# Weight conversion on VectorE instead of GpSimd, and three attention transposes on TensorE, in an attention and two-MoE kernel

## The chip, the cores and the metric

The kernel runs on one core of one Trainium2 chip. The metric is the device time of one execution in microseconds (us). Three runs of the kernel before took 1321.39 to 1324.82 us, with a median of 1322.66.

A core has a matrix engine (TensorE, PE in the rows), three engines for elementwise work (VectorE = DVE, ScalarE = ACT, GpSimd = POOL) and a queue that issues DMAs (SyncE = SP). Each runs its own list of instructions in order, and they wait for each other through semaphores.

## The reference

```python
# attention: q, k, v are (4, 8, 768, 64); 8 memory keys stand before each window
for c in range(nc):                       # chunks of 32 queries
    c_start, c_end = c * 32, c * 32 + 32
    l_start, r_end = max(0, c_start - 16), min(S, c_end + 8)
    k_full = concatenate([mem_k, k[:, :, l_start:r_end]], axis=2)
    v_full = concatenate([mem_v, v[:, :, l_start:r_end]], axis=2)
    scores = scale * matmul(q[:, :, c_start:c_end], k_full.T)
    a = exp(scores - max(scores))
    out[:, :, c_start:c_end] = matmul(a / (sum(a) + 1e-9), v_full)
x = out.transpose(0, 2, 1, 3).reshape(3072, 512)
# first MoE: 512 -> 2048 -> 512
h = x @ w_in
x = (maximum(h, 0) + log1p(exp(-abs(h)))) @ w_out
# second MoE: 512 -> 1536 -> 512
y = ((x @ w_a) * (x @ w_b)) @ w_out2
```

The weights lie in memory as 64-bit floats; everything else is 32-bit.

## The kernel before

**Numbers in two parts.** A large product is made of three matmuls with operands that are rounded to the type fp32r: high by high, high by low, low by high. So each operand, a weight as well as an activation, is split once: ScalarE copies it into the rounded type (high part), another engine subtracts this from the value (low part). For the activations g of the first MoE that is `split`, with ScalarE at L443 and GpSimd at L444; for x, ScalarE at L317 or L413 and VectorE at L318 or L414.

**Converting a weight.** A tile of 128x512 weights arrives as pairs of 32-bit words (raw). `convert_a` makes a 32-bit float (tmp) of it: ScalarE handles the high words (L104), VectorE shifts the low words (L106) and joins the two (L107). `convert_b` splits that: ScalarE makes the high part (L114), GpSimd the low part (L115). There are two tmp buffers, so the next L106 waits for the L115 two tiles before. 32 tiles belong to the first MoE, 36 to the second.

**Stages.** The 3072 tokens go in 8 tiles of 384. Phase 1 does the attention and the first MoE, phase 2 the second MoE; in between the result x1 is written to memory and read again.

- First the tokens of tile 0 are attended in six blocks of 64 queries (class Block, the table ROUND), while the first weights are loaded and converted. How many loads stand ahead of each block's own loads on SP is in EARLY_RAW, and W_BY has those behind the blocks.
- Then come the tiles t = 0 to 7 of phase 1. Each takes 16 steps f: twelve matmuls make ph (`emit_h`, L454), ScalarE makes three activations of it (L460 to L462), VectorE joins them to g (L464), g is split, and twelve matmuls bring it into four accumulators px (`emit_x1`, L477). px of step f - 2 stands behind ph of step f (LAG = 2), and ph has two banks. So g must be split within about one group of twelve matmuls.
- Meanwhile the next tile's three units of 128 queries are attended (class Unit). A unit's steps are: turn (VectorE transposes k and q with 32x32 stream transposes, L355 to L361, and ScalarE adds the memory keys, L363), scores (TensorE, L374), soft (VectorE's reductions L327, ScalarE's eight exponentials L331), norm (VectorE L335 and L336, then the product L338, for units on GpSimd), flip and flip2 (ten stream transposes by VectorE of the attention weights into af, L392), values (TensorE, L406) and place (x's two parts, L413 and L414).
- During tile 0 the rest of the first MoE's weights are converted too (1.5 tiles per step, CV_AT), and the loads run AHEAD tiles ahead. In the last tile, t = 7, and in phase 2's first tile, it is the second MoE's weights. x for phase 2 is loaded and split in `load_x1` (L491, VectorE L493, GpSimd L494). At the end of a tile the accumulators are copied out (xo, L482) and stored.
- In phase 2 a step makes two groups of twelve (`emit_ab`, L509), their product c (ScalarE L516, VectorE L518), its split, and twelve matmuls into y (`emit_y`, L529).

**What sets the order.** Up to the end of tile 0 each engine's list is just the order in which the code is written. From tile 1 on only TensorE's and VectorE's lists are, the others come from a scheduler, and in phase 2 only TensorE's. A plan places the units: a slot is half a step (2f before px, 2f + 1 behind it), and the tables STEPS and EARLY_STEPS give each step's distance from the unit's place. The three units attended during tile 0 (numbers 3, 4 and 5, here called unit 1, 2, 3) use EARLY_STEPS with a place of their own, EARLY_AT + EARLY_BY * i. SP loads k and q for the next tile after the last unit's turn (L187, L189), and in the last part of tile 0 it also issues the first loads that stay for phase 2.

A unit's attention weights after the softmax (sm) have queries on the 128 partitions and keys along the row; `values` wants keys on the partitions (af), hence the flip. The blocks before tile 0 do this with four transposes on TensorE against an identity matrix, ident (L303), and a copy by ScalarE.

## Time and profile before

| | before |
|---|---|
| median of 3 runs | 1322.66 us |
| the profiled execution | 1324.25 us |
| its span | 1322.4 us |
| TensorE busy | 1242.5 us, 94% |
| VectorE busy | 486.7 us, 37% |
| ScalarE busy | 530.9 us, 40% |
| GpSimd busy | 405.6 us, 31% |

The span goes from the first to the last instruction of the trace; the execution's own time holds 1.85 us more around it. A share of busy time is a mean over stages: tile 0 begins at 50.41 us, tile 1 at 167.17, the last tile at 629.54. From 723.75 on only the second MoE's work is left, where the y of its first step begins. In tile 0 each of the four engines is busy for a half to three quarters of the time; from tile 1 to tile 6 and in phase 2 TensorE is busy nearly all the time and the others for a small part.

### The profile page before, as it was taken

The page shows a single profiled execution, that of the slowest core. Times are in us where ns is not written, and L with a number is a line of the kernel's source. Part 1 is how long each engine was busy: PE and PEld are TensorE (multiplying, and loading weights), DVE is VectorE, ACT ScalarE, POOL GpSimd, SP SyncE. Part 2 cuts the span into 40 slices and gives each one's busy share as a digit, 9 for nine tenths or more (in the row PEclk, how much of TensorE's full clock was granted, in tenths as well). Part 3 has the DMA queues.
Part 4 walks back from the last instruction along what each step waited for, and adds up shares of the span by engine and source line. Part 5 has one row for each costly group of instructions (what it writes and reads, how often), then busy time and mean ns, then how long its engine had stood idle before and what let it go on. Part 6 is the DMA issues. An engine that isn't in the chain of part 4 may idle for free.

```text
span 1322.4 us, 20143 instructions
## 1 busy us (share of the span) xinstructions
PE 1242.5 (94%) x7848; PEld 1173.3 (89%) x7848; DVE 486.7 (37%) x1199; ACT 530.9 (40%) x1322; POOL 405.6 (31%) x348
## 2 busy tenths in 40 slices
PE   5767799999999999999798999999999999999998
PEld 3667789999999999999787999999999999999997
DVE  5677744544444454444778511110111011010100
ACT  4655656556556556554675311111111111111111
POOL 2454522323322322323677521121212121121111
PEclk9688889999999999999999999999999999999999
DMA  8962411213141311311765000010100001000000
GB/s 189 204 215 70 83 42 34 64 27 57 36 73 36 58 50 31 66 22 42 238 201 191 7 25 25 0 48 1 48 1 32 18 0 49 0 24 1 24 1 24
DMA packets 170170, 77.99 MB, mean 59 GB/s; under 512 B 137691, under 2 KB 162395, under 8 KB 170075
## 3 DMA queue, kind: packets, MB, share of 16 engines
q1 hardware_dynamic: 169563, 76.64, 22.0%
q8 instruction: 61, 1.00, 0.3%
q14 instruction: 34, 0.28, 0.1%
q0 software_dynamic: 512, 0.07, 0.0%
HBM read 64.09 MB, written 12.58 MB: 58 GB/s over the span
## 4 chain that ended last, share of the span: by engine, by line
PE 79%; DVE 5%; issue 5%; POOL 4%; SPq 3%; ACT 2%; DMA 1%; DVEq 0%; POOLq 0%; ACTq 0%
PE pab L509 30%; PE ph L454 16%; PE py L529 15%; PE px L477 15%; POOL w L115 3%; DVE tmp L106 2%; DVE tmp L107 2%; PE sc L374 1%; SPq L269 1%; PE pxa L406 1%; ACT w L114 1%; ACT e L461 1%; SPq L266 0%; ACT e L462 0%; SPq L89 0%
## 5 line engine op out<-in xcount | busy, mean ns | idle before, releaser
L509 PE MATMUL pab<-x,w 128*128 128x384 f32 x2304 | 418.9, 337 | 0.3 <-PE px L477 0.3
L509 PEld LDWEIGHTS pab<-x,w 128*128 128x128 f32 x2304 | 405.7, 188 | 9.2 <-PE px L477 0.6
L454 PE MATMUL ph<-x,w 128*128 128x384 f32 x1536 | 299.8, 344 | 16.3 <-ACT x L413 6.8
L454 PEld LDWEIGHTS ph<-x,w 128*128 128x128 f32 x1536 | 273.3, 192 | 23.6 <-ACT x L413 7.8
L518 DVE TENSOR_TENSOR c<-pab,a 128x384 f32<-128x384 f32 x96 | 53.5, 557 | 498.8 <-PE pab L509 497.8
L464 DVE SCALAR_TENSOR_TENSOR g<-ph,e 128x384 f32<-128x384 f32 x128 | 71.1, 556 | 250.5 <-ACT e L462 241.1
L516 ACT COPY a<-pab 128x384 f32<-128x384 f32 x96 | 46.1, 480 | 249.0 <-PE pab L509 249.0
L115 POOL TENSOR_TENSOR w<-tmp,w 128x512 fp32r<-128x512 f32 x68 | 101.5, 1496 | 104.4 <-ACT w L114 74.1
L460 ACT ACTIVATE e<-ph 128x384 f32<-128x384 f32 x128 | 62.0, 484 | 121.4 <-PE ph L454 109.5
L392 DVE STREAM_TRANSPOSE af<-sm 32x256 f32<-32x256 f32 x210 | 91.2, 434 | 3.0
L107 DVE SCALAR_TENSOR_TENSOR tmp<-raw,tmp 128x512 uint32<-128x512 uint32 x68 | 77.5, 1141 | 11.0 <-ACT raw L104 6.8
L106 DVE SCALAR_TENSOR_TENSOR tmp<-raw,zero 128x512 uint32<-128x512 uint32 x68 | 71.8, 1058 | 20.7 <-POOL w L115 18.4
L461 ACT ACTIVATE e<-e 128x384 f32<-128x384 f32 x128 | 67.1, 525 | 3.6
L462 ACT ACTIVATE e<-e 128x384 f32<-128x384 f32 x128 | 67.0, 524 | 3.7
L331 ACT ACTIVATE sm<-sm,st 128x96 f32<-128x96 f32 x168 | 60.5, 362 | 14.5 <-DVE st L327 14.5
L114 ACT CAST w<-tmp 128x512 fp32r<-128x512 f32 x68 | 41.8, 614 | 46.0 <-DVE tmp L107 46.0
L338 POOL TENSOR_TENSOR sm<-sm,st 128x768 f32<-128x768 f32 x21 | 32.2, 1536 | 60.1 <-DVE st L336 46.9
L104 ACT ACTIVATE raw<-raw 128x512 f32<-128x512 f32 x68 | 45.7, 672 | 6.6 <-DMA raw<-in_moe_w_in_dram 4.4
L406 PEld LDWEIGHTS pxa<-af,vn 96*64 96x64 f32 x672 | 23.1, 143 | 19.2 <-DVE af L392 9.7
L406 PE MATMUL pxa<-af,vn 96*64 96x64 f32 x672 | 26.5, 233 | 13.5 <-DVE af L392 9.2
L327 DVE CUSTOM_DVE_ANT_0 sm<-sc,mask 128x96 f32<-128x96 f32 x168 | 31.4, 252 | 6.5 <-PE sc L374 6.5
L374 PEld LDWEIGHTS sc<-kt,qt 64*64 64x64 f32 x672 | 17.2, 147 | 18.1 <-DVE x L414 7.5
(220 smaller groups left out, 1883.5 us busy)
## 6 DMA issues: line engine op xcount, KB each, us to landing
raw<-in_moe_w_out_dram SPq DMA_DIRECT2D x28, 512.0 KB
raw<-in_moe_w_in_dram SPq DMA_DIRECT2D x16, 512.0 KB
vn<-in_v_dram SPq DMA_DIRECT2D x35, 176.0 KB
raw<-in_moe_w_a_dram SPq DMA_DIRECT2D x12, 512.0 KB
x_scratch<-xo SPq DMA_DIRECT2D x32, 192.0 KB
xr<-x_scratch SPq DMA_DIRECT2D x8, 768.0 KB
raw<-in_moe_w_b_dram SPq DMA_DIRECT2D x12, 512.0 KB
out_dram<-yo SPq DMA_DIRECT2D x24, 256.0 KB
```

The source lines that it names most:

```text
L106: nc.vector.scalar_tensor_tensor(val, low, 29, zero.to_broadcast([P, 512]), ALU.logical_shift_right, ALU.bitwise_or)
L107: nc.vector.scalar_tensor_tensor(val, high, 3, val, ALU.logical_shift_left, ALU.bitwise_or)
L115: nc.gpsimd.tensor_tensor(w[:, 1], val, w[:, 0].bitcast(F32), ALU.subtract)
L392: nc.vector.transpose(out=af[32 * kb:32 * kb + 32, x], in_=self.sm[32 * x:32 * x + 32, :, 32 * kb:32 * kb + 32])
L406: nc.tensor.matmul(px[64 * j:64 * j + 64, i, QB * w:QB * w + QB], lhsT=vn[:, w, 2 * i + j], rhs=af[:, 2 * w:2 * w + 2, KT * j + i], start= ...
L454: nc.tensor.matmul(ph, lhsT=a, rhs=c, start=n == 0, stop=n == 3 * KT - 1)
L461: nc.scalar.activation(e, e, AF.Exp, scale=-1.0)
L462: nc.scalar.activation(e, e, AF.Ln, bias=1.0)
L464: nc.vector.scalar_tensor_tensor(g, ph, 0.0, e, ALU.max, ALU.add)
L477: nc.tensor.matmul(acc[t][i][:, :TT], lhsT=a, rhs=c, start=f == 0 and m == 0, stop=f == NF1 - 1 and m == 2)
L509: nc.tensor.matmul(p, lhsT=a, rhs=c, start=n == 0, stop=n == 3 * KT - 1)
L529: nc.tensor.matmul(acc[t][i], lhsT=a, rhs=c, start=f == 0 and m == 0, stop=f == NF2 - 1 and m == 2)
```

## The change

- The low part of a weight (old L115) is made by VectorE. GpSimd takes no part in a conversion.
- VectorE's first step of a conversion (old L106) has one source tensor instead of two: the OR with a tile of zeros is dropped, and with it that tile.
- `split` takes an engine. The low part of g is made by VectorE in tile 0 and in the last tile of phase 1, that of c in phase 2's first tile; GpSimd keeps them elsewhere.
- `emit_soft` takes two callbacks: `one` stands between VectorE's g and ScalarE's high part, `two` between the high part and the low part. The second conversion of an odd step, which stood behind the split as a whole, is now spread around it.
- The three units attended during tile 0 get norm_v (their product on VectorE) and flip_p: eight transposes by TensorE against ident into two banks, and two copies by ScalarE, instead of ten stream transposes by VectorE. The steps' distances and the units' places change a little, and in the loads ahead of the blocks three of the six numbers are smaller by one, with one more behind them.

```diff
-EARLY_STEPS = ((-7.5, "turn"), (-5.3, "scores"), (-5.2, "soft"), (-4, "norm"), (-2, "flip"), (0, "flip2"),
-               (2, "values"), (2.9, "place"))
-EARLY, EARLY_AT, EARLY_BY = 3, 14, 8.5
+EARLY_STEPS = ((-7.5, "turn"), (-5.3, "scores"), (-5.2, "soft"), (-3, "norm_v"), (-1.5, "flip_p"),
+               (1, "values"), (2, "place"))
+EARLY, EARLY_AT, EARLY_BY = 3, 14.5, 8.25
-EARLY_RAW = (0, 1, 2, 4, 6, 8)
-W_BY = (2, 2, 2, 2)
+EARLY_RAW = (0, 1, 2, 3, 5, 7)
+W_BY = (3, 2, 2, 2)
...
-        nc.vector.scalar_tensor_tensor(val, low, 29, zero.to_broadcast([P, 512]), ALU.logical_shift_right, ALU.bitwise_or)
+        nc.vector.tensor_scalar(val, low, 29, None, ALU.logical_shift_right)
         nc.vector.scalar_tensor_tensor(val, high, 3, val, ALU.logical_shift_left, ALU.bitwise_or)
...
-        nc.gpsimd.tensor_tensor(w[:, 1], val, w[:, 0].bitcast(F32), ALU.subtract)
+        nc.vector.tensor_tensor(w[:, 1], val, w[:, 0].bitcast(F32), ALU.subtract)
...
+        def norm_v(self):
+            normalize(nc.vector, self.sm, self.st)
+
+        def flip_p(self):
+            for j in range(2):
+                pa = ps.tile([P, 512], F32, tag="att", name=f"pa{j}_{self.u}")[:KB].rearrange("p (i t) -> p i t", i=KT)
+                for i in range(KT):
+                    nc.tensor.transpose(pa[:, i], self.sm[:, KT * j + i], ident)
+                nc.scalar.copy(af[:, :, KT * j:KT * j + KT], pa.rearrange("p i (x s) -> p x i s", x=4))
...
-    def split(val, name):
+    def split(val, name, engine=nc.gpsimd, between=None):
...
         nc.scalar.copy(hi, val)
-        nc.gpsimd.tensor_tensor(lo, val, hi.bitcast(F32), ALU.subtract)
+        if between:
+            between()
+        engine.tensor_tensor(lo, val, hi.bitcast(F32), ALU.subtract)
...
-    def emit_soft(t, f, ph, between=None):
+    def emit_soft(t, f, ph, engine=nc.gpsimd, one=None, two=None):
...
-        if between:
-            between()
-        gt[t, f] = split(g, f"g{t}_{f}")
+        if one:
+            one()
+        gt[t, f] = split(g, f"g{t}_{f}", engine, two)
...
-        ct[t, f] = split(c, f"c{t}_{f}")
+        ct[t, f] = split(c, f"c{t}_{f}", nc.vector if t == 0 else nc.gpsimd)
...
+                    more = n_cv[0] + 1 < due
                     convert_1(0)
-                    emit_soft(t, f, ph, partial(convert_1, 1))
-                    while n_cv[0] < due:
-                        convert_1(0)
-                        convert_1(1)
-                    if due == len(uses):
+                    emit_soft(t, f, ph, nc.vector, partial(convert_1, 1), partial(convert_1, 0) if more else None)
+                    if more or due == len(uses):
                         convert_1(1)
...
+                    more = f % 2
                     convert_2(0)
-                    emit_soft(t, f, ph, partial(convert_2, 1))
-                    if f % 2:
-                        convert_2(0)
+                    emit_soft(t, f, ph, nc.vector, partial(convert_2, 1), partial(convert_2, 0) if more else None)
+                    if more:
                         convert_2(1)
```

Line numbers of the kernel after are those of before less 2 up to the class Unit (L104 becomes L102, L106 and L107 become L104 and L105, L114 and L115 become L112 and L113), 9 more from `values` on (L406 becomes L415, L443 becomes L452) and 11 more from the low part in `split` on (L444 becomes L455, L464 becomes L475). The new transposes are L404, their copies L405.

In the rows that follow, a name carries its own number in the program behind its tile's or step's number (g_5_912 is the g of step 5 in tile 0).

VectorE in tile 0, from unit 1's normalization (st) to its flip (af), before: tmp is a weight in conversion, g an activation.

```order
L335 TENSOR_SCALAR st_811<-st_811 128x8
L336 RECIPROCAL st_811<-st_811 128x8
L106 SCALAR_TENSOR_TENSOR tmp_904<-raw_663,zero 128x512
L107 SCALAR_TENSOR_TENSOR tmp_904<-raw_663,tmp_904 128x512
L464 SCALAR_TENSOR_TENSOR g_5_912<-ph_5_887,e_5_908 128x384
L106 SCALAR_TENSOR_TENSOR tmp_921<-raw_665,zero 128x512
L107 SCALAR_TENSOR_TENSOR tmp_921<-raw_665,tmp_921 128x512
L392 STREAM_TRANSPOSE af<-sm_810 32x256 x5
L106 SCALAR_TENSOR_TENSOR tmp_960<-raw_708,zero 128x512
L107 SCALAR_TENSOR_TENSOR tmp_960<-raw_708,tmp_960 128x512
L464 SCALAR_TENSOR_TENSOR g_6_968<-ph_6_945,e_6_964 128x384
L392 STREAM_TRANSPOSE af<-sm_810 32x256 x5
```

The same stretch after; w is a weight's low part, g_5l an activation's, sm the attention weights.

```order
L475 SCALAR_TENSOR_TENSOR g_5_907<-ph_5_882,e_5_903 128x384
L113 TENSOR_TENSOR w_909<-tmp_817,w_909 128x512
L104 TENSOR_SCALAR tmp_915<-raw_663 128x512
L105 SCALAR_TENSOR_TENSOR tmp_915<-raw_663,tmp_915 128x512
L455 TENSOR_TENSOR g_5l<-g_5_907,g_5h 128x384
L113 TENSOR_TENSOR w_920<-tmp_899,w_920 128x512
L333 TENSOR_SCALAR st_853<-st_853 128x8
L334 RECIPROCAL st_853<-st_853 128x8
L336 TENSOR_TENSOR sm_852<-sm_852,st_853 128x768
L104 TENSOR_SCALAR tmp_965<-raw_706 128x512
L105 SCALAR_TENSOR_TENSOR tmp_965<-raw_706,tmp_965 128x512
L475 SCALAR_TENSOR_TENSOR g_6_973<-ph_6_950,e_6_969 128x384
```

The ten stream transposes and two conversions between them are gone from VectorE; one product over sm (L336), two low parts of weights and one of g are there instead, and the low part of g_5 stands behind a whole conversion.

TensorE at the same flip, before: px are the accumulators of the first MoE, fed by g.

```order
L477 MATMUL px_3_738<-g_3l,w_643 128x384
L477 MATMUL px_3_738<-g_3h,w_643 128x384
L454 MATMUL ph_6_945<-x_397,w_677 128x384 x12
L477 MATMUL px_0_735<-g_4h,w_688 128x384
L477 MATMUL px_0_735<-g_4l,w_688 128x384
```

TensorE there after; pa are the two banks that take the transposed sm.

```order
L488 MATMUL px_3_728<-g_3l,w_641 128x384
L488 MATMUL px_3_728<-g_3h,w_641 128x384
L404 MATMUL pa_3_938<-ident,sm_852 96x128 x4
L404 MATMUL pa_3_944<-ident,sm_852 96x128 x4
L465 MATMUL ph_6_950<-x_395,w_675 128x384 x12
L488 MATMUL px_0_725<-g_4h,w_686 128x384
```

The eight transposes stand ahead of ph_6, so ph_6 and all behind it wait for VectorE's product over sm.

ScalarE at the end of tile 0, before: e are the three activations of a step, raw_6703 the first weight for phase 2, x the third unit's attention result.

```order
L443 CAST g_14h<-g_14_1540 128x384
L114 CAST w_1549<-tmp_1532 128x512
L460 ACTIVATE e_15_1582<-ph_15_1569 128x384
L461 ACTIVATE e_15_1582<-e_15_1582 128x384
L462 ACTIVATE e_15_1582<-e_15_1582 128x384
L104 ACTIVATE raw_6703<-raw_6703 128x512
L443 CAST g_15h<-g_15_1586 128x384
L363 COPY kt_1593<-mem_t 128x4x8 x2
L413 CAST x_1059<-pxa_1612 128x4x128
```

ScalarE there after.

```order
L452 CAST g_14h<-g_14_1537 128x384
L112 CAST w_1546<-tmp_1529 128x512
L405 COPY af<-pa_5_1549 96x4x128
L405 COPY af<-pa_5_1555 96x4x128
L102 ACTIVATE raw_6707<-raw_6707 128x512
L471 ACTIVATE e_15_1586<-ph_15_1573 128x384
L472 ACTIVATE e_15_1586<-e_15_1586 128x384
L473 ACTIVATE e_15_1586<-e_15_1586 128x384
L452 CAST g_15h<-g_15_1590 128x384
L361 COPY kt_1597<-mem_t 128x4x8 x2
L422 CAST x_1071<-pxa_1604 128x4x128
```

raw_6707 is the weight that was raw_6703. It stood behind the activations of step 15 and now stands ahead of them, behind the two copies into af; it takes the buffer of ident, which the third unit's transposes now use, where it took an earlier one before.

VectorE at the start of phase 2, before: pab and c belong to phase 2, xo are copies of the last tile's accumulators.

```order
L107 SCALAR_TENSOR_TENSOR tmp_7836<-raw_7355,tmp_7836 128x512
L518 TENSOR_TENSOR c_0_7531<-pab_0_1_7516,a_0_7529 128x384
L106 SCALAR_TENSOR_TENSOR tmp_7843<-raw_7357,zero 128x512
L107 SCALAR_TENSOR_TENSOR tmp_7843<-raw_7357,tmp_7843 128x512
L106 SCALAR_TENSOR_TENSOR tmp_7850<-raw_7408,zero 128x512
L107 SCALAR_TENSOR_TENSOR tmp_7850<-raw_7408,tmp_7850 128x512
L106 SCALAR_TENSOR_TENSOR tmp_7900<-raw_7410,zero 128x512
L518 TENSOR_TENSOR c_1_7583<-pab_1_1_7568,a_1_7581 128x384
L482 COPY xo_0_7601<-px_0_6831 128x384
L107 SCALAR_TENSOR_TENSOR tmp_7900<-raw_7410,tmp_7900 128x512
L482 COPY xo_1_7604<-px_1_6832 128x384
```

VectorE there after.

```order
L455 TENSOR_TENSOR c_0l<-c_0_7535,c_0h 128x384
L113 TENSOR_TENSOR w_7483<-tmp_7478,w_7483 128x512
L104 TENSOR_SCALAR tmp_7847<-raw_7361 128x512
L105 SCALAR_TENSOR_TENSOR tmp_7847<-raw_7361,tmp_7847 128x512
L113 TENSOR_TENSOR w_7844<-tmp_7840,w_7844 128x512
L529 TENSOR_TENSOR c_1_7587<-pab_1_1_7572,a_1_7585 128x384
L104 TENSOR_SCALAR tmp_7854<-raw_7412 128x512
L113 TENSOR_TENSOR w_7851<-tmp_7847,w_7851 128x512
L493 COPY xo_0_7605<-px_0_6835 128x384
L105 SCALAR_TENSOR_TENSOR tmp_7854<-raw_7412,tmp_7854 128x512
L493 COPY xo_1_7608<-px_1_6836 128x384
```

Low parts of c and of weights now stand between the steps of the conversions, ahead of the c of the second step and of the copies xo.

## Rows read from the trace of the kernel before

**Rows 1.** Busy time by stretch; each engine's busy us, the clock, DMA share.

```profile
core 0: us, PE busy (x) PEld busy (x) DVE busy (x) ACT busy (x) POOL busy (x), PEclk, DMA share, GB/s
20.00:40.00 20.00, 12.38 (x130) 9.53 (x128) 10.97 (x48) 13.00 (x47) 4.18 (x4) 0.81 0.95 224
50.41:167.17 116.76, 86.01 (x553) 81.41 (x553) 87.91 (x168) 70.75 (x173) 62.90 (x52) 0.81 0.52 137
629.54:723.75 94.21, 80.38 (x432) 76.62 (x433) 73.29 (x77) 62.76 (x126) 68.31 (x45) 0.97 0.64 215
640.16:702.20 62.04, 57.19 (x313) 53.99 (x313) 46.74 (x50) 45.03 (x91) 44.25 (x30) 1.00 0.62 205
723.75:1322.40 598.65, 593.29 (x3096) 554.05 (x3096) 81.80 (x128) 107.45 (x215) 131.92 (x110) 0.99 0.05 19
```

**Rows 2.** The chain of waits in tile 1: start, us, what ran.

```profile
175.17 2.08 PE ph L454 x12
```

**Rows 3.** What TensorE waits for in tile 0: us, times, longest.

```profile
PE pxa L406 <- DVE af L392: 9.2, 3, 3.5
PE sc L374 <- DVE x L414: 7.0, 2, 3.7
```

**Rows 4.** Timeline of VectorE and GpSimd: start, us, line, operation.

```profile
40.19 0.56 DVE L338 TENSOR_TENSOR work<-work 128x384 f32<-128x384 f32 x1
...
52.34 0.41 DVE L318 TENSOR_TENSOR x<-pxb,x 128x256 fp32r<-128x256 f32 x1
...
70.23 0.67 DVE L361 STREAM_TRANSPOSE qt<-qn 128x512 f32<-128x512 f32 x1
...
75.52 1.73 POOL L115 TENSOR_TENSOR w<-tmp,w 128x512 fp32r<-128x512 f32 x1
...
76.21 1.58 DVE L107 SCALAR_TENSOR_TENSOR tmp<-raw,tmp 128x512 uint32<-128x512 uint32 x1
...
79.14 0.68 DVE L106 SCALAR_TENSOR_TENSOR tmp<-raw,zero 128x512 uint32<-128x512 uint32 x1
...
623.56 0.96 DVE L493 CAST x<-xr 128x1536 fp32r<-128x1536 f32 x1 [4.18 <-DMA xr<-x_scratch]
```

**Rows 5.** VectorE's lines in tile 0: busy, mean ns, idle before and releaser.

```profile
L107 DVE SCALAR_TENSOR_TENSOR tmp<-raw,tmp 128x512 uint32<-128x512 uint32 x25 | 28.6, 1142 | 7.7 <-ACT raw L104 5.4
L106 DVE SCALAR_TENSOR_TENSOR tmp<-raw,zero 128x512 uint32<-128x512 uint32 x25 | 25.9, 1037 | 12.8 <-POOL w L115 12.7
```

**Rows 6.** Timeline of TensorE, with the idle time before and its releaser.

```profile
27.89 0.61 PE L303 MATMUL pat<-ident,work 128*96 128x128 f32 x4 [0.47 <-DVE work L338]
...
33.87 1.49 PE L280 MATMUL pt<-ident,qk 96*128 96x96 f32 x8 [3.94 <-DMA qk<-in_mem_k_dram]
...
108.30 1.54 PE L374 MATMUL sc<-kt,qt 64*64 64x96 f32 x28 [3.66 <-DVE x L414]
109.77 4.21 PE L454 MATMUL ph<-x,w 128*128 128x384 f32 x12
...
636.44 0.53 PE L477 MATMUL px<-g_0h,w 128*128 128x384 f32 x1 [4.54 <-DVE xo L482]
...
723.75 1.19 PE L529 MATMUL py<-w,c_0h 128*128 128x512 f32 x2 [4.41 <-ACT c_1h L443]
```

**Rows 7.** Timeline of ScalarE and VectorE around unit 1's exponentials.

```profile
78.00 0.38 ACT L331 ACTIVATE sm<-sm,st 128x96 f32<-128x96 f32 x1 [3.00 <-DVE st L327]
...
80.89 0.65 ACT L104 ACTIVATE raw<-raw 128x512 f32<-128x512 f32 x1
81.44 0.47 ACT L460 ACTIVATE e<-ph 128x384 f32<-128x384 f32 x1
...
83.05 0.56 DVE L464 SCALAR_TENSOR_TENSOR g<-ph,e 128x384 f32<-128x384 f32 x1 [0.79 <-ACT e L462]
```

**Rows 8.** Timeline of SP's queue and ScalarE at the end of tile 0.

```profile
132.81 0.33 SPq L187 DMA_DIRECT2D kn<-in_k_dram  x1
...
153.36 0.47 SPq L189 DMA_DIRECT2D qn<-in_q_dram  x1
...
161.01 0.39 SPq L89 DMA_DIRECT2D raw<-in_moe_w_a_dram  x1
...
165.33 0.67 ACT L104 ACTIVATE raw<-raw 128x512 f32<-128x512 f32 x1 [1.27 <-DMA raw<-in_moe_w_a_dram]
```

More of the change, by code (lines that the diff above doesn't have):

```diff
@@ L80, in attn_moe_moe2 @@
     n_w = [0]
-    zero = mp.tile([P, 1], U32, tag="zero", name="zero", bufs=1)
-    nc.vector.memset(zero, 0)
     def fetch(dst, key, src):
```

## The prediction

> **What bounds the kernel now.** I first read the busy time by stretch [rows 1]. Phase 2 behind 723.75 is TensorE almost without a gap (593.29 of 598.65 us), and the tiles between the first and the last of phase 1 run on it too (a group of twelve matmuls each 2.08 us in the chain of waits [rows 2]); the change leaves their work alone. What can be gained lies in two stretches. Tile 0, from 50.41 to 167.17, takes 116.76 us, of which TensorE is idle 116.76 - 86.01 = 30.75, at a mean granted clock of 0.81. The last tile with the start of phase 2, 629.54 to 723.75, has 94.21 - 80.38 = 13.83 us idle, of which 62.04 - 57.19 = 4.85 lie in its steady part.
>
> Then I read what TensorE waits for in tile 0 [rows 3]: above all at the attention steps, for VectorE (af 9.2, x 7.0 us). VectorE is late because of its neighbour: L107 takes 1.58 us where it runs beside GpSimd's L115, while L106 without such company takes 0.68 [rows 4], and the 25 of each in tile 0 have means of 1.04 and 1.14 us, with 12.7 us of waiting until L115 releases a buffer [rows 5]. After each long wait TensorE runs at the lower of its two levels (1.2 GHz) for a while: twelve matmuls took 4.21 instead of 2.08 us behind a wait for x [rows 6].
>
> **Prices.** Steps on an engine that is not waiting follow each other some 0.1 us closer than their durations. For ScalarE: eight exponentials 2.89 (78.00 to 80.89), L104 0.55, and 1.61 from the first of the three activations to VectorE's g [rows 7]. For VectorE: 0.62 for L107 and for the low part of a weight that comes from GpSimd (128x384 of that form took 0.56 [rows 4]; at 0.95 ns a column, which this row and the 0.68 of L106's 512 give, it is 0.68 in duration); 0.49 each for g and its low part; the turn 1.6 (two transposes at 0.67 and a half one); normalization of 128x768 0.9 by the same slope. The new L106 has one source tensor. The trace shows no such form in this size: above it is bounded by the two-source L106, 0.68, below by the one-source L493, 0.96 for 1536 columns [rows 4]; with the 0.2 fixed that the two-source rows leave, L493 gives 0.5 ns a column, so 0.46 for 512. I take 0.5 with its gap, since L493 is the row of its kind; the other end is 0.79. The Trainium skill (VectorE: DVE Perf Modes, The perf-mode tier table) has one-source fp32 work in SBUF at two elements a cycle and two-tensor work at one; an estimate from it is 0.43 us. L493 agrees, and with that price the sum below would be some 1 us lower.
>
> A conversion thus costs VectorE 0.5 + 0.62 + 0.62 = 1.74, where L106 and L107 alone cost it 2.18 beside GpSimd. A step of f has 1.5 conversions, so 2.61 + 0.98 = 3.6 us, below TensorE's 2 x 2.08 = 4.16.
>
> **Before tile 0.** One 512 KB weight load less stands ahead of block 5. TensorE waited 3.94 us for that block [rows 6]; at the 224 GB/s of this stretch [rows 1] the load is 2.3 us, of which 2.2 show. Low parts now stand ahead of the reductions of two rounds and take back 0.5. Gain 1.7, between 0 and 2.3.
>
> **Tile 0.** No engine's sum bounds it, so I follow the chain. VectorE's last x of the blocks ended at 52.75 [rows 4]. Without contention (0.9) and the wait for a buffer (0.6), with L106 shorter (0.3), a low part more (0.6) and the 1.7, that is 49.9. From there to the end of unit 1's normalization VectorE issues 11 conversions (19.1), six g and six low parts (5.9), the turn with mem_t (1.8), reductions (1.4) and normalization (1.4): 29.6 us, and about 5.4 of waiting, of which 1.9 because ScalarE's L104 stands behind the eight exponentials. So flip 1 starts at 84.9. TensorE needs ten groups at 2.08, the scores and some lower clock up to there: about 74. **The new wait is at the flip**, 11 us long. Queued behind it on TensorE is ph_6 and all that follows; in the old order the transposes stood on VectorE and let ph_6 and ph_7 pass.
>
> From flip 2 to flip 3, in us behind its start: transposes to 2.1 at the lower clock (four took 0.61 at full [rows 6]), px_8 and ph_11 to 7.8; ScalarE's three and g_11 to 10.0; low part, L104, L105, two more low parts to 12.9; turn to 14.5, x to 15.5; e_12 begins behind kt, x and L102 at 15.35, g_12 ends at 17.5; low parts to 18.6, exponentials to 21.8, L102 to 22.35, g_13 at 24.5, five more VectorE steps to 27.3, normalization to 28.7. TensorE reaches the flip at 24.6 and waits 4.1. From flip 1 to flip 2 the same chain has a group more behind the flip: 30.8. So flip 3 starts at 84.9 + 30.8 + 28.7 = 144.4.
>
> **The end of tile 0 has a second wait that grows.** ScalarE's first raw of phase 2 (raw_6707) now stands ahead of e_15; it stood behind it. Its DMA is on SP behind the k and q loads of the next tile, which were issued from 132.81 to 153.8, 21 us behind the third turn, and takes 4.3 from issue to use [rows 8]. Turn 3 ends 14.5 behind flip 2, at 130.2; so the data is there at 130.2 + 21 + 0.4 + 4.3 = 155.9, 11.5 behind flip 3, while ph_15 is done 7.7 behind it. From there L102, the activations, g_15, its cast and low part, turn, kt and the x cast make 5.5, and the first ph of tile 1 starts at 161.4. It started at 167.17: gain of head and tile 0 **5.8**. At ph_12 to ph_14 it was about 14; the third flip and this DMA give 8 of it back.
>
> A page speaks against the transposes: the Trainium skill (TensorE: Matmul & The Clock Gate, Part 4: PE-mode transpose) gives about 275 ns for one of 128x128 inside a kernel. The row has 0.15 us each at full clock; 24 at the page's price would cost about 3 us more on the path, and the sum would be 1309. The row decides.
>
> **The last tile.** VectorE needs 3.6 and ScalarE about as much for a step of f that took TensorE 62.04 / 13 = 4.77 [rows 1]. Without waits it is 26 groups at 2.1 = 54.6; I leave 1.5 for the split of the second x, which stays on GpSimd: 56.1, gain 5.9. At the start the copies of px stand behind two more low parts: TensorE waited 4.54 there [rows 6] and I add 0.9. At the start of phase 2 it waited 4.41 for c_1h [rows 6], because VectorE's c_1 stood behind L106 and L107 that waited for GpSimd, and then ran at the lower clock (2.5 us longer). In the new order c_1 and xo_0 are ready within a microsecond of their inputs, ahead of py_0: gain 6.9, less 0.8 for what is late next (the low part of c_1, behind two copies). Sum **11.1**, between 4 and 14.
>
> Together 16.9: span 1322.4 - 16.9 = 1305.5. The profiled run took 1324.25, its span and 1.85 around it, 1.6 more than the median of 1322.66; from the median the forecast is 1306.
>
> **Rivals.**
> More gain: VectorE keeps up with TensorE at the second and third flip, and the raw does not hold ScalarE. For it: the sum of VectorE's steps in tile 0 is only some 73 us. Against it: the chain above is latency, not busy time. Then the 14 us of ph_14 stay and the last tile gives 13: 1296.
> Tile 0 gains nothing: each flip waits like the first, or the one-source L106 costs 0.79 (3.2 us more up to flip 1, about 1 in each period). Then the last tile alone pays: 1312.
> GpSimd is not out of the way: the splits of x that remain there, and ScalarE's order in the last tile, which no table writes, keep that tile's waits. All of its gain goes: 1317.
> Slower: VectorE becomes the bound of both stretches. Place: the three steps of a conversion on one engine in order. Price: if each costs what L106 does on the average now, 1.04 us, a conversion is 3.1 and a step of f 1.5 x 3.1 + 0.98 = 5.6 against 4.77 now, 11 us for the last tile, and 11 x 1.38 = 15 up to the first flip: 11 + 15 - 5.8 = 20, of which I take half to be hidden in waits, 1333. It decides from 2.5 us a conversion on. Against it: the long durations are those beside GpSimd.
>
> **How the numbers follow.** Forecast 0.5, more gain 0.2, nothing in tile 0 0.15, nothing in the last tile 0.07, slower 0.08. The range is 1294 to 1319: from more gain with the low ends of its costs to the case without the last tile; beyond lie the slower case and tails. About 0.3% (4 us) is what can be told from no change: faster by more 0.87, within it 0.06, slower by more 0.07.
>
> **What would show it.** In the changed profile: GpSimd without an instruction in tile 0; L105 (the old L107) at 0.69 throughout; VectorE's L104 near 0.46; TensorE waiting for VectorE's sm at the transposes, 11, 4 and 4 us; ScalarE waiting 3 to 5 us for raw_6707 ahead of e_15; tile 1 starting near 161; the last tile's groups without waits, and py_0 without the 4.41. It is wrong if the flips don't wait, if L104 is 0.68, or if waits for g remain in the last tile.

## The result, and the profile after

The kernel after took 1311.78 us (median of 4 runs, 1311.32 to 1312.14) against 1323.74 for before: a ratio of 0.991, 95% interval 0.9892 to 0.9929. The forecast was 1306. The profiled execution took 1311.32 us with a span of 1309.5, so the span is 12.9 us shorter than before, where 16.9 were forecast.

First the busy time by stretch after, cut where the same work begins and ends as in [rows 1]: tile 0 from its first full group of twelve, the last tile's 26 groups, from there to the first py, and the rest.

```profile
core 0: us, PE busy (x) PEld busy (x) DVE busy (x) ACT busy (x) POOL busy (x), PEclk, DMA share, GB/s
53.05:160.98 107.93, 82.14 (x576) 77.90 (x576) 73.66 (x179) 72.22 (x177) 3.71 (x7) 0.88 0.53 142
634.96:692.48 57.52, 56.79 (x313) 54.28 (x312) 43.18 (x78) 44.90 (x89) 1.22 (x1) 0.99 0.69 220
692.48:714.90 22.42, 18.29 (x96) 18.32 (x97) 19.17 (x33) 11.46 (x23) 2.55 (x1) 0.92 0.58 202
714.90:1309.50 594.60, 589.12 (x3097) 551.20 (x3096) 81.83 (x143) 106.33 (x213) 106.60 (x90) 1.00 0.05 18
```

Tile 0's first full group began at 52.81 before and at 53.05 after, so nothing was gained ahead of it. Tile 0 itself went from 114.36 to 107.93, the last stretch from 598.65 to 594.60. The 26 groups were 62.07 with their waits; they are 57.52, but a new wait of 4.13 follows.

VectorE's lines in tile 0 answer to [rows 5]. No step of a conversion is stretched beside GpSimd any more, and the wait for GpSimd is gone.

```profile
L113 DVE TENSOR_TENSOR w<-tmp,w 128x512 fp32r<-128x512 f32 x25 | 17.2, 688 | 0.0
L105 DVE SCALAR_TENSOR_TENSOR tmp<-raw,tmp 128x512 uint32<-128x512 uint32 x24 | 16.6, 693 | 11.6 <-ACT raw L102 9.6
L104 DVE TENSOR_SCALAR tmp<-raw 128x512 uint32<-128x512 uint32 x24 | 10.1, 422 | 0.4
```

TensorE's timeline has the three flips and the end of tile 0; its waits there were af and x before [rows 3].

```profile
88.06 1.91 PE L404 MATMUL pa<-ident,sm 128*96 128x128 f32 x8 [11.02 <-DVE sm L336]
...
119.17 1.05 PE L404 MATMUL pa<-ident,sm 128*96 128x128 f32 x8 [2.50 <-DVE sm L336]
...
145.46 1.91 PE L404 MATMUL pa<-ident,sm 128*96 128x128 f32 x8 [3.86 <-DVE sm L336]
...
160.98 0.44 PE L465 MATMUL ph<-x,w 128*128 128x384 f32 x1 [4.10 <-ACT x L422]
```

The last wait comes from the first weight of phase 2, as SP's queue and ScalarE show. In [rows 8] ScalarE waited 1.27 for it, behind step 15's activations; now 6.11, ahead of them.

```profile
151.30 0.41 SPq L87 DMA_DIRECT2D raw<-in_moe_w_a_dram  x1
...
155.06 0.66 ACT L102 ACTIVATE raw<-raw 128x512 f32<-128x512 f32 x1 [6.11 <-DMA raw<-in_moe_w_a_dram]
```

At the two ends of the last tile, VectorE, GpSimd and TensorE (the last rows of [rows 6] are TensorE's counterparts):

```profile
617.10 3.56 POOL L505 TENSOR_TENSOR x<-xr,x 128x1536 fp32r<-128x1536 f32 x1 [4.83 <-PE px L488]
...
617.34 3.87 DVE L105 SCALAR_TENSOR_TENSOR tmp<-raw,tmp 128x512 uint32<-128x512 uint32 x1
...
630.98 0.66 PE L488 MATMUL px<-g_0h,w 128*128 128x384 f32 x1 [6.87 <-DVE xo L493]
...
691.26 3.77 POOL L505 TENSOR_TENSOR x<-xr,x 128x1536 fp32r<-128x1536 f32 x1 [70.60 <-DVE x L504]
...
691.64 3.67 DVE L104 TENSOR_SCALAR tmp<-raw 128x512 uint32<-128x512 uint32 x1
...
695.96 0.55 DVE L475 SCALAR_TENSOR_TENSOR g<-ph,e 128x384 f32<-128x384 f32 x1
...
696.61 5.97 PE L520 MATMUL pab<-x,w 128*128 128x384 f32 x24 [4.13 <-issue]
...
714.90 0.63 PE L540 MATMUL py<-w,c_0h 128*128 128x512 f32 x2
```

L104, 0.42 us in tile 0, took 3.67, until GpSimd's split of the second x ended. So g of step 14 came 3.3 us late, and the first products of phase 2 need the bank of ph that this g frees. The trace names no releaser for their wait ("issue"); they start 0.10 us behind the end of this g here and in e4, e7 and e12 below. The wait that stood at py (4.41 before) is gone.

The kernel before has both hold-ups too, in its old lines, at the same two splits. But at the start of phase 2 its g of step 14 (at 701.58) stood well ahead of the step that was held, and TensorE did not wait there:

```profile
624.66 3.82 POOL L494 TENSOR_TENSOR x<-xr,x 128x1536 fp32r<-128x1536 f32 x1 [5.88 <-DVE x L493]
625.16 3.87 DVE L107 SCALAR_TENSOR_TENSOR tmp<-raw,tmp 128x512 uint32<-128x512 uint32 x1
...
701.58 0.54 DVE L464 SCALAR_TENSOR_TENSOR g<-ph,e 128x384 f32<-128x384 f32 x1
...
707.25 3.97 POOL L494 TENSOR_TENSOR x<-xr,x 128x1536 fp32r<-128x1536 f32 x1
...
707.77 4.00 DVE L106 SCALAR_TENSOR_TENSOR tmp<-raw,zero 128x512 uint32<-128x512 uint32 x1
```

### The profile page after: what moved, and what is told of

It is laid out like the page before. It is cut to its first block, busy times and chain, and to the rows that moved or that the text cites. A ratio compares the mean times of both kernels' runs of the same rounds, so it can differ in the third digit from the quotient of the medians.

```text
span 1309.5 us, 20027 instructions
## 1 busy us (share of the span) xinstructions
PE 1237.2 (94%) x7872; PEld 1170.1 (89%) x7872; DVE 473.4 (36%) x1283; ACT 534.7 (41%) x1328; POOL 247.6 (19%) x233
## 4 chain that ended last, share of the span: by engine, by line
PE 84%; DVE 5%; SPq 3%; ACT 3%; DMA 3%; issue 1%; DVEq 0%; ACTq 0%
PE pab L520 31%; PE ph L465 18%; PE px L488 17%; PE py L540 15%; DMA raw<-in_moe_w_out_dram 2%; PE sc L372 1%; PE pxa L415 1%; SPq L267 1%; DVE w L113 1%; DVE tmp L105 1%; ACT e L472 1%; SPq L264 1%; ACT e L471 1%; ACT e L473 1%; DVE g L475 0%
## 5 line engine op out<-in xcount | busy, mean ns | idle before, releaser
L475 DVE SCALAR_TENSOR_TENSOR g<-ph,e 128x384 f32<-128x384 f32 x128 | 71.2, 557 | 257.0 <-ACT e L473 253.3
L390 DVE STREAM_TRANSPOSE af<-sm 32x256 f32<-32x256 f32 x180 | 78.2, 435 | 2.5
L505 POOL TENSOR_TENSOR x<-xr,x 128x1536 fp32r<-128x1536 f32 x8 | 28.4, 3554 | 153.5 <-DVE x L504 148.7
L105 DVE SCALAR_TENSOR_TENSOR tmp<-raw,tmp 128x512 uint32<-128x512 uint32 x68 | 50.2, 739 | 14.4 <-ACT raw L102 11.0
L113 DVE TENSOR_TENSOR w<-tmp,w 128x512 fp32r<-128x512 f32 x68 | 46.9, 689 | 16.9 <-ACT w L112 16.8
L102 ACT ACTIVATE raw<-raw 128x512 f32<-128x512 f32 x68 | 45.4, 673 | 15.4 <-DMA raw<-in_moe_w_in_dram 7.1
L112 ACT CAST w<-tmp 128x512 fp32r<-128x512 f32 x68 | 41.6, 613 | 17.2 <-DVE tmp L105 17.1
L195 POOL DMA_DIRECT2D mem_n<-in_mem_k_dram x16 | 8.9, 560 | 155.8 <-DVE mem_t L353 155.8
L336 POOL TENSOR_TENSOR sm<-sm,st 128x768 f32<-128x768 f32 x18 | 26.5, 1472 | 60.1 <-DVE st L334 46.9
L104 DVE TENSOR_SCALAR tmp<-raw 128x512 uint32<-128x512 uint32 x68 | 31.9, 469 | 5.0 <-DMA raw<-in_moe_w_in_dram 4.6
L329 ACT ACTIVATION_READ_ACCUMULATOR sm<-sm,st 128x1 f32 x168 | 31.4, 187 | 0.0
```

Of the source, the lines that this page charges most:

```text
L105: nc.vector.scalar_tensor_tensor(val, high, 3, val, ALU.logical_shift_left, ALU.bitwise_or)
L113: nc.vector.tensor_tensor(w[:, 1], val, w[:, 0].bitcast(F32), ALU.subtract)
L329: nc.scalar.activation(sm[:, h], sm[:, h], AF.Exp, bias=st[:, 0, h:h + 1], scale=-1.0, accum_out=st[:, 1, h:h + 1])
L390: nc.vector.transpose(out=af[32 * kb:32 * kb + 32, x], in_=self.sm[32 * x:32 * x + 32, :, 32 * kb:32 * kb + 32])
L475: nc.vector.scalar_tensor_tensor(g, ph, 0.0, e, ALU.max, ALU.add)
```

## The experiments

Times are medians of 4 to 10 runs, ratios are to the kernel before in the same job. The last three columns are from the profiled execution: the start of the first full group, tile 0 from there to tile 1's first ph, and from there to the end.

| run | us | ratio, 95% | starts | tile 0 | rest |
|---|---|---|---|---|---|
| before | 1323.7 | | 52.8 | 114.4 | 1155.2 |
| after | 1311.8 | 0.989–0.993 | 53.1 | 107.9 | 1148.5 |
| e1_conversion_only | 1308.7 | 0.988–0.991 | 51.1 | 104.7 | 1149.9 |
| e2_flips_only | 1326.5 | 1.001–1.003 | 52.2 | 118.6 | 1154.5 |
| e3_loads_old | 1312.1 | 0.990–0.993 | 50.9 | 107.8 | 1149.3 |
| e4_x_split_vector | 1306.7 | 0.986–0.989 | 52.2 | 109.0 | 1144.1 |
| e5_two_sources | 1320.1 | 0.996–0.998 | 50.6 | 111.2 | 1155.4 |
| e6_scalar_by_hand | 1305.0 | 0.984–0.988 | 51.0 | 106.6 | 1145.9 |
| e7_g_low_gpsimd | 1306.2 | 0.985–0.990 | 50.5 | 109.3 | 1143.9 |
| e10_flip_later | 1297.3 | 0.978–0.983 | 50.8 | 95.9 | 1148.9 |
| e11_stream_later | 1304.8 | 0.984–0.987 | 51.0 | 103.5 | 1148.6 |
| e12_x_split_pieces | 1304.8 | 0.984–0.987 | 51.7 | 112.0 | 1142.6 |
| b1_later_x_scalar | 1290.4 | 0.973–0.976 | 50.2 | 93.7 | 1143.4 |
| b2_one_more | 1292.0 | 0.973–0.977 | 51.0 | 97.0 | 1141.8 |

Two limits. The work ahead of the first full group is the same in after, e1, e4, e6, e7 and e10 to b2, and it began between 50.2 and 53.1, latest in after: up to some 3 us of a difference between two totals can come from there. And after, e4 and e12 have the same lists up to the third flip, yet tile 0 took 107.9, 109.0 and 112.0. Of the 4.0 us between after and e12, 3.2 arose ahead of the third flip, 2.8 of them behind the second, where the same matmuls ran at another granted clock (the third number from the end). The rows are of after, e4 and e12:

```profile
119.17:124.34 5.17, 5.17 (x32) 4.92 (x32) 3.52 (x7) 2.04 (x4) 0.00 (x0) 1.00 0.01 2
118.04:124.76 6.72, 6.72 (x32) 6.47 (x32) 3.52 (x7) 2.04 (x4) 0.00 (x0) 0.75 0.01 1
118.24:125.98 7.74, 7.74 (x32) 7.42 (x33) 3.52 (x7) 2.05 (x4) 0.00 (x0) 0.64 0.00 1
```

So up to 4 us of a difference in tile 0 between two profiled executions need not come from the edit. The one of e12 took 1308.1, 3.3 above the median of its runs.

**The two halves of the change.** e1 puts the old steps of the early units back into the kernel after (tables EARLY_* and norm, flip, flip2) and keeps all else; e2 puts only the new steps into the kernel before.

```diff
-EARLY_STEPS = (... (-3, "norm_v"), (-1.5, "flip_p"), (1, "values"), (2, "place"))
+EARLY_STEPS = (... (-4, "norm"), (-2, "flip"), (0, "flip2"), (2, "values"), (2.9, "place"))
```

> The kernel after with the old attention steps of the three early units: GpSimd's product and VectorE's ten stream transposes, in the old places. All of the conversion, the splits of g and c and the loads stay as in the kernel after. Theory 1: the gain of tile 0 comes from taking GpSimd out of the conversion, and the transposes on TensorE add little, since TensorE waited 17.4 us at them; then tile 1 begins within 3 us of 161 and the time is 1309 to 1314 (the kernel after: 1311.8). Theory 2: VectorE's chain decides and the ten transposes (4.4 us a unit) are on it; then tile 1 begins 5 us or more later and the time is 1317 or more.

> The kernel before with only the new attention steps (product on VectorE, transposes on TensorE, the new distances and places). Conversion, splits and loads are those of the kernel before. Theory 1 (the gain is that of the conversion): TensorE waits at each flip for a VectorE that still runs beside GpSimd, tile 0 does not get shorter, 1321 to 1328. Theory 2 (the flips are on the chain that decides): tile 0 gets some 4 us shorter, about 1318.

e2 came out for theory 1; e1 lies beyond it, with tile 1 at 155.8, 5.2 earlier than after, where within 3 was expected. In tile 0 the change without the new steps of the units gains 9.7 us (114.4 to 104.7). The new steps lose 4.2 with the old conversion (118.6) and 3.2 with the new one. One profile each does not fix these two figures, by the 4 us above; that the new steps lose with the old conversion, the total of e2 shows (ratio 1.001–1.003). e1 also beats the kernel after in the total by 3.1, of which 2.0 is its earlier start. With VectorE's transposes TensorE waits at the values and not at a flip:

```profile
PE pxa L415 <- DVE af L390: 10.9, 3, 4.4
PE sc L372 <- DVE qt L359: 4.3, 1, 4.3
PE sc L372 <- DVE x L423: 4.3, 2, 2.4
```

**Is it the engine or the place?** e10 puts two slots more between each unit's scores and its new transposes: the first unit's transposes stand two slots later, the second's one later behind scores one earlier, and the third's where they were behind scores two earlier. e11 moves the values later with the old transposes.

```diff
-               (1, "values"), (2, "place"))     # flip_p at -1.5
-EARLY, EARLY_AT, EARLY_BY = 3, 14.5, 8.25
+               (3, "values"), (4, "place"))     # e10, flip_p at 0.5
+EARLY, EARLY_AT, EARLY_BY = 3, 16.5, 7.25
-               (2, "values"), (2.9, "place"))
-EARLY, EARLY_AT, EARLY_BY = 3, 14, 8.5
+               (3.5, "values"), (4.4, "place")) # e11, the old steps
+EARLY, EARLY_AT, EARLY_BY = 3, 15.5, 7.75
```

> The kernel after with the transposes of the first unit two slots later and of the second one slot later (a group of twelve of ph and one of px more pass ahead of the first), the third where it was. Theory 1: the transposes cost 3.3 us in tile 0 because ph and px stand behind a TensorE that waits for the product over sm; with more groups ahead the first wait falls from 11.0 to about 7 and tile 0 gets 2 to 4 us shorter, 1308 to 1310. Theory 2: the end of tile 0 is set by VectorE's and ScalarE's sum and the last loads, wherever TensorE waits: 1311 to 1313.

> As the run with the conversion alone (old stream transposes and GpSimd product for the early units; 1308.7), but with 1.5 slots more between the transposes and the values, and the three units at 15.5, 23.25 and 31 instead of 14, 22.5 and 31. Theory 1: what the run with the later transposes gained (14.5 us) came from the distance on TensorE between the scores and the step that needs the weights, whichever engine transposes; then this gains most of it too: tile 0 (104.7 us from the first full group to tile 1) gets to 96 to 100, 1299 to 1303. Theory 2: the transposes on TensorE are needed for it, since VectorE's 4.4 us a unit and the wait for GpSimd's product stay; 1306 to 1310.

e10 gained 14.5, far more than expected: 12.1 in tile 0 and 2.2 by its earlier start. The first wait fell by just the two groups of TensorE that now stand ahead (11.02 to 6.82), and the second and third flips did not wait at all, for their units too have two slots more between scores and flip:

```profile
PE pa L404 <- DVE sm L336: 6.8, 1, 6.8
PE pxa L415 <- issue: 4.9, 2, 3.2
PE ph L465 <- ACT x L422: 2.9, 1, 2.9
```

e11 shortened tile 0 by 1.2 only against e1: the waits moved from the values to the scores, which VectorE's turn releases.

```profile
95.83 1.56 PE L372 MATMUL sc<-kt,qt 64*64 64x96 f32 x32 [7.30 <-DVE qt L359]
...
122.92 1.56 PE L372 MATMUL sc<-kt,qt 64*64 64x96 f32 x32 [5.11 <-DVE qt L359]
```

So the transposes on TensorE pay, 8.8 us in tile 0 against e1, if TensorE has enough to do ahead of them. In the kernel after they stand two slots too near to their scores.

**The form of L104.** e5 takes the tile of zeros and the two-source form back.

```diff
-        nc.vector.tensor_scalar(val, low, 29, None, ALU.logical_shift_right)
+        nc.vector.scalar_tensor_tensor(val, low, 29, zero.to_broadcast([P, 512]), ALU.logical_shift_right, ALU.bitwise_or)
```

> The kernel after with L104 in its old form with two source tensors (the tile of zeros is back). Theory 1: the form costs 0.68 instead of 0.42 us, and VectorE's chain sets both stretches: 11 conversions up to the first flip make 2.9 us, the next two periods about 0.8 each, the last tile some 0.26 a conversion in its steady part (19 of them, 5 us); 1317 to 1321. Theory 2: VectorE has slack between its waits, and the 0.26 us are hidden outside the stretch up to the first flip: 1312 to 1315.

Theory 1, at its upper end. The mean of that step is 686 ns instead of 422; tile 0 is 3.3 us longer, and what follows it 6.9. Of the 12 us that the change gains, 8.3 are lost without this one line.

```profile
L106 DVE SCALAR_TENSOR_TENSOR tmp<-raw,zero 128x512 uint32<-128x512 uint32 x24 | 16.5, 686 | 0.4
```

**GpSimd's last pieces.** e7 gives the low parts of g and c back to GpSimd, e4 gives VectorE the low part of x for phase 2's first two tiles, e12 cuts it into four on GpSimd.

```diff
-                    emit_soft(t, f, ph, nc.vector, ...)          # e7, and gpsimd for c
+                    emit_soft(t, f, ph, nc.gpsimd, ...)
-        nc.gpsimd.tensor_tensor(x[:, 1], raw, ...)               # e4
+        (nc.vector if t < 2 else nc.gpsimd).tensor_tensor(x[:, 1], raw, ...)
+        for i in range(KT):                                      # e12
+            nc.gpsimd.tensor_tensor(x[:, 1, i], raw[:, i], ...)
```

> The kernel after with the low part of x for the first two tiles of phase 2 made by VectorE instead of GpSimd (three instructions' worth, 128x1536 each, some 1.8 us by the 0.69 of 128x512). Theory 1: TensorE's wait of 4.1 us at the first products of phase 2 is VectorE's L104, which took 3.67 instead of 0.42 beside GpSimd's 3.77 us subtraction; then L104 is back at 0.42, the wait falls to about 2.5 and the time to 1309 to 1310.5. Theory 2: the wait has another cause (ScalarE's order, the bank of ph); then VectorE only has more to do and the time is 1311.8 to 1314.

> The kernel after with GpSimd's low part of x in four instructions of 128x384 instead of one of 128x1536. Theory 1: a VectorE instruction that starts beside a GpSimd instruction ends only when that one has ended, so four short ones let VectorE through in between: L104's 3.67 falls to about 1.3, the next three are stretched to some 1.4 each, g is late by 2 to 2.5 instead of 3.3 us, TensorE's wait at phase 2's first products falls from 4.1 to about 3: 1309 to 1311. Theory 2: GpSimd holds VectorE off for as long as it has work, pieces or not: 1311.5 to 1313.

> The kernel after with the low parts of g and c back on GpSimd everywhere; weights stay on VectorE. Theory 1: any instruction of GpSimd's on two tensors holds VectorE's two-tensor and one-tensor steps up while it runs: 16 in tile 0 and 14 in the last tile, each with up to 1.0 us, less the 0.47 that VectorE no longer has: 1316 to 1322. Theory 2: only the weights' low parts (1.7 us, 25 of them, with a buffer that waits for them) mattered: 1310 to 1313.

e4: L104 was back at 0.42, the split took VectorE 1.75, and TensorE's wait fell to 2.44, as theory 1 has it.

```profile
690.30 0.42 DVE L104 TENSOR_SCALAR tmp<-raw 128x512 uint32<-128x512 uint32 x1
690.63 1.75 DVE L505 TENSOR_TENSOR x<-xr,x 128x1536 fp32r<-128x1536 f32 x1
...
692.90 0.55 DVE L475 SCALAR_TENSOR_TENSOR g<-ph,e 128x384 f32<-128x384 f32 x1
...
693.56 4.40 PE L520 MATMUL pab<-x,w 128*128 128x384 f32 x24 [2.44 <-issue]
```

But the gain of 4.4 behind tile 0 is about twice what was expected: the same hold-up at the start of the last tile (L105, 3.87 us beside L505) went too, and TensorE's first 24 matmuls of phase 2 took 4.40 instead of 5.97 behind the shorter wait. e12 came out for theory 1: with four short instructions each of VectorE's steps is late by one of them at most, TensorE waited 2.38 (about 3 expected), and as in e4 both ends of the last tile gained: 5.9 behind tile 0.

```profile
691.43 5.31 POOL L506 TENSOR_TENSOR x<-xr,x 128x384 fp32r<-128x384 f32 x4 [66.25 <-DVE x L504]
...
691.81 1.25 DVE L104 TENSOR_SCALAR tmp<-raw 128x512 uint32<-128x512 uint32 x1
693.09 1.36 DVE L105 SCALAR_TENSOR_TENSOR tmp<-raw,tmp 128x512 uint32<-128x512 uint32 x1
694.37 0.55 DVE L475 SCALAR_TENSOR_TENSOR g<-ph,e 128x384 f32<-128x384 f32 x1
```

e7 was expected to lose by theory 1 and gained 5.6. L104 did get slower in tile 0 (a mean of 707 ns), but the 109.3 of the tile against 107.9 can't be told from the spread above. Of the gain, 2.6 is the earlier start, and 4.6 came behind tile 0, because VectorE's order changed at the one place: g of step 14 now came ahead of the step that is held. TensorE waited 1.10 instead of 4.13, and its first 24 matmuls of phase 2 took 4.40 instead of 5.97.

```profile
691.77 0.55 DVE L475 SCALAR_TENSOR_TENSOR g<-ph,e 128x384 f32<-128x384 f32 x1
692.53 3.22 DVE L113 TENSOR_TENSOR w<-tmp,w 128x512 fp32r<-128x512 f32 x1 [0.22 <-ACT w L112]
```

So e7 says little on g's low parts; that they are better on VectorE everywhere is not shown.

**ScalarE's order.** e6 orders ScalarE by the code in all of phase 1.

```diff
-                early.enter_context(tc.manual_schedule(engines={engines["P"], engines["V"]}))
+                early.enter_context(tc.manual_schedule(engines={engines["P"], engines["V"], engines["S"]}))
```

> The kernel after with ScalarE's list in the order of the code in all of phase 1 (before: only up to tile 0). The first weight of phase 2 then stands in the last tile, and no longer ahead of step 15's activations in tile 0. Theory 1: its DMA (ScalarE waited 6.1 us for it) sets the end of tile 0; tile 1 then begins 3 to 4 us earlier after the third flip, and the time is 1306 to 1309. Theory 2: the end of tile 0 hangs on k's and q's loads for the next turn, which go through the same queue: less than 1 us. In the last tile the order by hand is the same as in tile 0: without the scheduler's mixing of conversions between the activations the steps of 4.56 us get nearer to 4.2, up to 4 us more; or, as rival, a load that is late holds the activations up and the last tile gets longer.

Theory 1 at both places. From the third flip to tile 1 it took 157.52 - 145.30 = 12.2 us instead of 15.5; the wait at px in the last tile fell from 6.87 to 4.73, and the 27 groups behind it, without the wait at their end, took 62.44 - 4.45 = 58.0 instead of 65.63 - 4.13 = 61.5. Tiles 1 to 6 gave 1.6 back and the part from phase 2's first products on 1.1; 2.1 of the total's 6.8 is the earlier start.

**The loads.** e3 has the old numbers.

```diff
-EARLY_RAW = (0, 1, 2, 3, 5, 7)
-W_BY = (3, 2, 2, 2)
+EARLY_RAW = (0, 1, 2, 4, 6, 8)
+W_BY = (2, 2, 2, 2)
```

> The kernel after with the old numbers for the loads ahead of the blocks. Theory 1: the stretch before tile 0 is bound by the transfers (DMA share 0.92 to 0.99), so moving a weight load only moved the wait from TensorE's block 5 to the third weight's conversion; the first ph starts within 0.7 us of 51.5 and the time is within 1.5 us of 1311.8. Theory 2 (as predicted): one load less ahead of block 5 is worth 1.7 us, so the old numbers give 1313.5.

In the total nothing can be told from the kernel after, as theory 1 has it and against the 1.7 of the prediction. But in its profile the first ph came at 49.41, 2.1 earlier than in after, where theory 1 allowed 0.7. In the kernel after ScalarE waits for the third weight, and block 4's reductions stand behind that conversion:

```profile
25.35 0.68 ACT L102 ACTIVATE raw<-raw 128x512 f32<-128x512 f32 x1 [2.57 <-DMA raw<-in_moe_w_in_dram]
```

**Together.** b1 has the edits of e10, e4 and e6, and b2 these two more:

```diff
-               (0.5, "flip_p"),
+               (1.5, "flip_p"),
...
-                    more = f % 2
+                    more = f % 2 and f > 1
```

> The kernel after with three edits that each gained alone: later transposes (-14.5), the first two splits of x on VectorE (-5.1), ScalarE by hand (-6.8). They lie in different places but for the end of tile 0, where later transposes have already moved step 15 and where the wait for the first weight of phase 2 was 2.9 us of TensorE; so 1297.3 - 5.1 - 3 to 5 = 1287 to 1290. If the gains are the same waits counted twice: 1292 or more.

> The combination of the three edits (1290.4) with the transposes one slot later still (all three units; the first wait was 6.9 us, so a group of twelve more covers 2.1 of it; those of the second and third did not wait), and with one weight's conversion less ahead of the copies xo in the last tile (its second conversion of step 1 is left out there and made up later; TensorE waited 5.2 us for xo, and the three VectorE steps and the low part make 1.7). Theory 1: both waits get shorter by these amounts: 1286 to 1288. Theory 2: the first flip's wait is a delay of the whole chain of VectorE and moves to the scores of the next unit and the values (2.6 and 1.7 us there now); then only the last tile gains, 1288 to 1290, and with a flip too near its values it gets slower, 1291 or more.

b1 is the fastest version, 1290.4, 21 us below the kernel after: the gains add up, less some 5, just above the range that was expected. b2 is not faster, as its theory 2 has it: the wait at px fell from 5.24 to 2.07, but tile 0 got 3.3 us longer. The first flip waited only 1.26; the next unit's scores, now right behind each flip, waited for ScalarE's copies to free their bank:

```profile
95.15 2.02 PE L372 MATMUL sc<-kt,qt 64*64 64x96 f32 x32 [3.79 <-ACT af L405]
...
120.65 2.03 PE L372 MATMUL sc<-kt,qt 64*64 64x96 f32 x32 [5.00 <-ACT af L405]
```

## Why the prediction was right, and where it was not

**The number.** The measured 1312 is also the number of the rival in which tile 0 gains nothing. That rival did not happen: the start and tile 0 together gave 6.2, where 5.8 were forecast, and what was missing was missing in the last tile.

**Prices: right.** L104 takes 0.42 in tile 0 (0.5 was taken; the estimate from the Trainium skill (VectorE: DVE Perf Modes, The perf-mode tier table) was 0.43, and the trace agrees). L105 and the low part are 0.69 there.

**Before tile 0: failed.** "Gain 1.7, between 0 and 2.3", and a last x at 49.9: it was 53.0, 3.1 late. TensorE's wait of 3.94 for block 5 [rows 6] went, as forecast, but a wait of ScalarE, 2.57, came. The transfers of this stretch were busy for 0.95 of the time [rows 1], so a load that is moved may only change who waits; e3 agrees, since the old loads cost nothing in the total. How much of the 3.1 is the loads is not shown: nine other kernels with the same list ahead of tile 0 began it at 50.2 to 52.2.

**Tile 0: right in the waits, with luck in the sum.** From the start to the first flip 35.0 us were forecast and 35.0 measured; the next periods 30.8 and 28.7, measured 31.1 and 26.3; the waits 11, 4 and 4, measured 11.0, 2.5 and 3.9. The load that holds ScalarE was there at 155.1 (155.9 forecast), and tile 1 began at 161.0 (161.4). ScalarE waited 6.1 for that load, where 3 to 5 were forecast. The third period and the stretch behind its flip (15.5 us, 17.0 forecast) made up what the head had lost, and that is luck: the 26.3 go with a granted clock of 1.00 behind the second flip, and with the same lists at 0.75 and 0.64 the period took 28.0 (e4) and 29.1 (e12), around the 28.7 of the forecast. What the sum did not ask is what the old flips would have cost with the new conversion: by e1 some 3.2 us less. "The new wait is at the flip" was the thing to price as an edit of its own.

**The last tile: failed, in one term.** Forecast 11.1, measured 12.9 - 6.2 = 6.7. The start came out (0.9 to be lost; from tile 1's start to the last tile's fourth ph it was 6.2 - 5.2 = 1.0). The start of phase 2 gained 3.2 up to py and 4.1 behind it, 7.3 where 6.1 were forecast. The failed term is "without waits it is 26 groups at 2.1 = 54.6; I leave 1.5 for the split of the second x": the groups took 57.5, and the split 4.1. So 5.9 forecast became 0.4. e4 and e12 show the second half: the split holds VectorE for its whole length, at a step ahead of a g that TensorE waits for. The old list had this g ahead of the held step (701.58 and 707.77 above); the new list turned the two round, and the prediction did not look for that. e6 shows the first half: with ScalarE's list by hand the 26 groups took 54.3, and the excess was gone. The prediction had named both causes (the third rival) and given them 0.07. One of its signs of being wrong, waits for g in the last tile, did appear.

**Other cost ends.** The two-source price was kept as the end that leads to 1312; e5 measured 1320. I had counted 3.2 us up to the first flip, where 1.6 were measured (36.6 against 35.0), and nothing behind tile 0, where it cost most (6.9).

## What to carry to other kernels

A step that one engine in order takes from another (here a transpose that needs a softmax) has two prices, its own and that of all that queues behind it: before moving it to the busiest engine, count how much work stands between the producer's start and the wait, and move the step back behind more of it. There is a limit: in b2 the step had moved so far that the next consumer waited instead. When an engine is cleared of most of its work, look at the last long instruction left there and at what its neighbour runs beside it, and ask whether the new order put a step that others wait for behind the one that is held. Where a long chain of short steps sets the pace, a cheaper form of one step pays although its engine is idle for a third of that stretch (73.7 of 107.9 us busy in tile 0): in e5 0.26 us a step made 8.3 us.

## What the runs showed of the hardware

While GpSimd's subtraction of two tensors runs, a step of a conversion on VectorE that starts behind its start ends only behind its end: 3.67 us for the one-source L104 (0.42 alone), 3.87 for the two-source L105 (0.69 alone), 1.25 and 1.36 beside pieces of a quarter. In e7 a low part of g on GpSimd and an L104 began together at 94.60: L104 took its 0.43, and GpSimd took 1.30, where it takes about 1.0 alone. Not every VectorE instruction is held. In e12 VectorE's g, which reads one operand from PSUM, took 0.55 in the middle of the same stretch, as it does alone. And a stream transpose, which has one source, in SBUF, ended ahead of the GpSimd instruction beside it. All 180 of its kind in tiles 1 to 6 of the kernel after took 0.42 to 0.44 us, beside GpSimd or not:

```profile
178.52 1.01 POOL L455 TENSOR_TENSOR g_2l<-g,g_2h 128x384 fp32r<-128x384 f32 x1 [1.25 <-ACT g_2h L452]
178.69 0.43 DVE L390 STREAM_TRANSPOSE af<-sm 32x256 f32<-32x256 f32 x1
```

The Trainium skill (SBUF — State Buffer, SBUF: two separate sides) says that the two engines' shared ports are locked for a whole instruction, by a GpSimd instruction or by a VectorE one that reads two SBUF inputs or uses the two-port mode, and are not split; the trace agrees.

Eight transposes of a unit took 1.05 us where the granted clock was 1.00 (2.4 GHz) and 1.91 where it was 0.50 (1.2 GHz), 0.13 and 0.24 us each:

```profile
88.06:89.97 1.91, 1.91 (x9) 1.82 (x10) 0.18 (x1) 0.58 (x1) 0.00 (x0) 0.50 0.69 228
119.17:120.22 1.05, 1.05 (x9) 1.05 (x10) 0.95 (x3) 0.00 (x0) 0.00 (x0) 1.00 0.00 0
```

TensorE had waited 11.0 us ahead of the first and 2.5 ahead of the second. The Trainium skill (TensorE: Matmul & The Clock Gate, Part 4: PE-mode transpose) gives about 275 ns for one in a kernel; the trace stays below that either way. The 24 took 4.9 us, the waits ahead of them 17.4.

Still open is why the same instructions reach the first full group at 50.2 in one kernel and at 53.1 in another; the transfers there are busy nearly all the time (0.95 before), and no run took one away. Open too is why the clock behind the second flip was granted differently to the same lists, and how the 9.7 us that tile 0 gained without the flips part between GpSimd's leaving the conversion and the one-source form: e5 puts the form alone at 3.3 in that tile.
